# One-core attention and gated-MLP kernel: Q and K loads in two requests each, Q in three fixed buffers, new orders of work, last head's transfers on GpSimd

## The chip, the cores and the metric

The kernel runs on one core of one Trainium2 chip. The metric is the device time of one execution in microseconds (us); the time of before is the median of three runs. One further execution was recorded by the hardware profiler, and it is this one that the rows of the profile describe. The engines are named as the profile names them: PE (TensorE, matmul), DVE (VectorE), ACT (ScalarE), POOL (GpSimd), SP (SyncE, which here only issues transfers). SP's requests are worked off by 16 DMA engines; each request is split over several of them.

## The reference

Two branches work on the same input x (2048 positions, 448 features) and are mixed by a gate of one number per position:

```python
g = sigmoid((x * gate_w).sum(-1, keepdims=True))
# a: attention with 16 heads of 28 features
qkv = (x @ wqkv).reshape(B, S, 3, H, 28).transpose(2, 0, 3, 1, 4)
scores = einsum("bhqd,bhkd->bhqk", q, k) * 28 ** -0.5
a = (softmax(scores) @ v).transpose(0, 2, 1, 3).reshape(B, S, 448) @ wo
# b: MLP with 1792 hidden features
gate, up = x @ W_gate, x @ W_up
b = (where(gate > 0, gate, 0) * up) @ W_down
out = g * a + (1 - g) * b
```

## The kernel before, in words

**Number format.** Every matmul factor is split into a high and a low part, and products are made of several terms of parts. For the scores of a head the terms are stacked as rows: a K buffer has four blocks of 28 rows (high, low, high, low part of K), and a Q buffer has four blocks of 28 rows (high, high, low, low part of Q), each 2048 wide, 8 KB to a row in f32. So one matmul with 112 rows sums four terms. Sixteen more rows carry the subtraction of the row maximum: -1 in K, and in Q two rows of maxima (written late by POOL) and zeros, which are loaded from `z_d`.

**Opening.** The projections to q and k (`qk`, L435) and to v (`vproj`, L453) run as a list of 35 items in alternation. Results go to DRAM, `qk_d` with the high part first and the low part second (outermost index 0 and 1). K and Q of head 0 are loaded ahead of item 0, those of head 1 ahead of item 6. From item `first` = 11 on, `AHEAD` = 102 matmuls of the maximum search for head 0 and 1 are mixed in (`smax`, L240 on PE and L241 on DVE).

**Rounds.** Then come 32 rounds, two to a head. A string of letters (`FIRST`, `SECOND`, `AA`, `BB` and so on) gives the order in which PE is fed in a round: `s` scores of the current head with exp on ACT (L263, L265), `m` maximum search for a head further on (L240, L241), `r` and `d` raw scores and their maxima for the last four key tiles of the next head (L271 to L279), `e` the exp of those, `x` a matmul of the MLP's gate and up projection (L608). The digit is the PSUM bank. PE works strictly in this order: when one `m` has to wait for its K or Q, all that is behind it waits as well.

**Between the rounds.** Behind the second round of head h stand, in this order: `load_k(h + 3)` (L217, four requests of 28 rows), `raw_top(h + 1)` (a maximum made on DVE, L284 to L292, sent to DRAM by `mr_d<-V`, L293, and back to all partitions by `V<-mr_d`, L294), `load_q(h + 3)` (L222, four requests of 28 rows, and L224, sixteen rows of zeros), then the next gate and up weights (`wgr<-wgu`, L316) and v (L639). All of these are issued by SP, which works in order as well: a request that waits for its buffer or its data holds up those behind it. The transfers of one queue are worked off in order on each DMA engine too. A K buffer comes free behind the last scores of its head, a Q buffer likewise. Q buffers come from a pool of three, which two x tiles and the first weight pair share in the opening.

**End.** When the attention is done the last head is normalised (`row_sums`, `spread`, `normalise`, L658 to L675): reciprocals are sent to DRAM, spread back over 32 partitions each, multiplied, and the head's output goes to `o_d`. Then the list `todo` runs the MLP's down projection (`down`, L888) with the attention's output projection (`wout`, L842) and the results mixed in.

Of the kernel before, what the change touches and what calls it, by code (L numbers as in the profile page):

```python
# [9 lines left out]
F32 = mybir.dt.float32  # L10
# [31 lines left out]

AHEAD = 102

# [3 lines left out]

FIRST = ("m2m3m6m7s0s1uxxxxs0xm2lxxxxUs3xs6xm1xxm7s0s2xxxs3m1xm0xxm2r7r3r1xxdr0s2dr7xdxxs3xdr2xs1m0ds3xxm1xm0s"
         "3r2xxm1ds3xm0xxm1xr3xs2m0dxxm1s2xx")  # L50

SECOND = ("xs0m1r2xm6s7dxs3m0xs1m6xs7xm3r2s0xm1dxs6m7xs3m0xs1r6xm2s3dxm7s1xm0s2xr3m1xs7dm2xs0m1xs7xm3r0s2xs7dm1"
          "xm3s2xs0m7xm1xs2r3xm0xds2m1xs0xs2m3xs0m1xr2s3m0xds1xxm3m0s1s2xxm3s1r0m2xm3ds1xs2xxm1xm2s0x")

AA = ("xs0r1m2xs6m7xxm3s0xm1s6xr2s7xm0dxs3m6xxm1s7r0xm3xds2xs6xm7xs1er3m2m0xm7s1exdm2xs0xm1er7xs0m3xdes2xxm"
      "0s1xem3r2xs1xdm0exxs3m1xs2exm0m3xs1m2exs0xr1m3exs2dm0xxs3xm1s2xm0xxr1m2s0d")

# [10 lines left out]

AZ = ("xs0xs1xxs2xxs6xs7xxs3xs0xxs1xxs2xs7xxs3xs0xxs1xxs2xs3xxs0xxs1xes2xxs3xes0xxs1xxes2xs0xxs1xx")

BZ = ("xs0xs1xxs2xxs6xs7xxs3xs0xxs1xxs2exs7xxs3xes0xxs1xxes2xs3xxs0exxs1xs2xexs3xs0xxs1xxs2xs0xxs1xx")

DA = ("xs0m1xr2m6s7xm3xs0xm2r7xs1m6dxs0xm3xs2xs1xm6r0m7xm2s3dxxm1s7xs3r2xm0m7xds3xs1m0xr3m7xs1dxes2m0xxm1xe"
      "s3m2xs0xr1em3xs2dxm0xes3xm2r1xs0em3dxs2xm0exs3xm2s1xem0r3xm2s1dxm0xxm2s1")
# [4 lines left out]
CA = ("xs0xm1s2r6m7xm3xs0xm2r6s1xxdm7s0m3xr2xs1m6dxs0xm7m3xs1xr6xm0xds2m7xs1xr3m0s2xdxm1m7xs0r2xem3s1dxm0s7"  # L79
      "xes3m1xm2xm0exs3r1xxm2des3xm0xs2m3exs1xr2m0exm3ds1xm0xexs3m1xs2xs0xxm2m1s0")  # L80

# [19 lines left out]
def gated_mix_kernel(ctx, tc, x, wq, wo, wgu, wd, out):  # L101
# [82 lines left out]
    K = [vp.tile([P, S], F32R, name=f"K{r}") for r in range(3)]  # L184

    def p_slot(k, name, dt=F32):
        return (vp if k < 5 else att).tile([P, 4, TB], dt, name=name, tag=f"P{k}", bufs=1)
# [3 lines left out]
    def slot(k):  # L191
        if k not in slots:
            slots[k] = p_slot(k, f"P_{k}")
        return slots[k]
# [14 lines left out]

    def q_slot(name):  # L210
        return vp.tile([P, 4, TB], F32R, name=name, tag="Q", bufs=3)

    Q = {}

    def load_k(h):
        for r in range(4):
            nc.sync.dma_start(f32(K[h % 3])[DH * r:DH * (r + 1)], qk_d[r % 2, 2 * DH * h:2 * DH * h + DH, :])  # L217

    def load_q(h):
        Q[h] = q_slot(f"Q_{h}").rearrange("p j t -> p (j t)")  # L220
        for r in range(4):
            nc.sync.dma_start(f32(Q[h])[DH * r:DH * (r + 1)], qk_d[r // 2, 2 * DH * h + DH:2 * DH * (h + 1), :])  # L222

        nc.sync.dma_start(f32(Q[h])[GD:], z_d[0:1].to_broadcast([P - GD, S]))  # L224

# [83 lines left out]
    def fetch_f(i):  # L309

        if i == 0:
            pair.append(vp.tile([P, 4, TB], F32, name="pair", tag="Q", bufs=3))
            WR[i] = pair[0][:, :2].rearrange("p s (c f) -> p s c f", c=4)
        else:
            WR[i] = fe.tile([P, 2, 4, P], F32, name=f"wgr_{i}", tag="wgr", bufs=2)
        nc.sync.dma_start(WR[i], wgu[i % NF])  # L316


    with tc.tile_pool(name="qkv", bufs=1) as pa:
# [75 lines left out]
        for tb in range(NB - 1, 0, -1):  # L395
            X[tb] = tuple(q_slot(f"X{r}_{tb}") if tb + r == NB else p_slot(next(free), f"X{r}_{tb}", F32R)
                          for r in range(2))

# [134 lines left out]
        spills = {15 + 3 * k: (NB - 1 - k // 2, k % 2) for k in range(6)}  # L533
        m, first, ahead = 0, 11, AHEAD
        for n, (f, *a) in enumerate(mixed):
# [105 lines left out]
    def pv(i0, ni, po):  # L641
# [11 lines left out]
        if (i0 + ni) % NK == 0:  # L653
            LS[h] = fe.tile([P, 16], F32, name=f"ls_{h}", tag="ls", bufs=2)
            nc.gpsimd.dma_start(LS[h], OS[h][DH::32].rearrange("j (p c) -> j p c", c=16))

    def row_sums(h):

        r = fe.tile([P, 16], F32, name=f"rs_{h}", tag="rs", bufs=2)
        nc.vector.reciprocal(r, LS.pop(h))  # L660
        nc.sync.dma_start(l_d[h].rearrange("j (p c) -> (j p) c", c=16), r)

    def spread(h):


        LS[h] = fe.tile([P, TB + 8], F32, name=f"rb_{h}", tag="rb", bufs=1)[:, :TB]
        for j in range(NB):
            nc.sync.dma_start(LS[h][32 * j:32 * j + 32], l_d[h][j:j + 1].to_broadcast([32, TB]))

    def normalise(h):  # L670
        o = OS.pop(h)
        engine = nc.gpsimd if h + 1 < H else nc.vector
        engine.tensor_tensor(o, o, LS.pop(h), op=OP.mult)
        for j in range(NB):
            nc.sync.dma_start(o_d[DH * h:DH * (h + 1), j * TB:(j + 1) * TB], o[32 * j:32 * j + DH])  # L675

# [5 lines left out]
    def small_things(h):  # L682

        load_v(h + 1) if h + 1 < H else None
        if h == 0:
            pack_wo()

# [3 lines left out]

    summed = []
    split_f(0, act_high, pool_low, (0,))
# [4 lines left out]
    for r, order in enumerate(ROUNDS):  # L698
# [91 lines left out]
        pv(i0, 8, banks[3])  # L790
    assert raw == NI and m == len(MAXIMA), (raw, m)
    stk.close()

# [22 lines left out]
    def fetch_o(tb):  # L816
        OR[tb] = r = pf.tile([P, 4, TB], F32, name=f"or_{tb}", tag="or", bufs=1)
        t = slice(tb * TB, (tb + 1) * TB)
        nc.sync.dma_start(r[:, 0:3], o_d[0:3 * P, t].rearrange("(c p) t -> p c t", p=P))
        for a in (0, 64):  # L820
            nc.sync.dma_start(r[a:a + 64, 3], o_d[3 * P:, t])

# [92 lines left out]

    todo = [(gate_up, done), (row_sums, H - 1), (gate_up, done + 1)]
    for i in range(NB * NF):
# [7 lines left out]


    before(0, (spread, H - 1))
# [62 lines left out]
```

## Time and profile before

| | |
|---|---|
| median of three runs | 1311.88 us (1309.97 to 1313.3) |
| profiled execution, its time | 1312.3 us |
| its span (first to last instruction) | 1310.5 us |
| PE busy | 1252.3 us, 96% of the span |
| DVE, ACT, POOL busy | 905.4, 841.7, 632.3 us |
| mean granted TensorE clock | 0.980 |
| moved by DMA | 159.14 MB, 121 GB/s on average |

PE is the engine to look at. Its busy time counts the modelled length of matmuls, which overlap, so a short wait of PE shows in the list of waits and in the timeline sooner than in the busy share. In the timeline and the windows, times are microseconds from the start of the span; a window row gives the length, then busy time and count of PE, PEld, DVE, ACT and POOL, then the granted clock (1.00 is full speed), the mean busy share of the 16 DMA engines, and GB/s.

### The profile page before, as it was taken

The page shows a single profiled execution, that of the slowest core. Times are in us where ns is not written, and L with a number is a line of the kernel's source. Part 1 is how long each engine was busy: PE and PEld are TensorE (multiplying, and loading weights), DVE is VectorE, ACT ScalarE, POOL GpSimd, SP SyncE. Part 2 cuts the span into 40 slices and gives each one's busy share as a digit, 9 for nine tenths or more (in the row PEclk, how much of TensorE's full clock was granted, in tenths as well). Part 3 has the DMA queues.
Part 4 walks back from the last instruction along what each step waited for, and adds up shares of the span by engine and source line. Part 5 has one row for each costly group of instructions (what it writes and reads, how often), then busy time and mean ns, then how long its engine had stood idle before and what let it go on. Part 6 is the DMA issues. An engine that isn't in the chain of part 4 may idle for free.

```text
span 1310.5 us, 18847 instructions
## 1 busy us (share of the span) xinstructions
PE 1252.3 (96%) x6447; PEld 865.9 (66%) x6447; DVE 905.4 (69%) x1446; ACT 841.7 (64%) x1661; POOL 632.3 (48%) x698
## 2 busy tenths in 40 slices
PE   9999698999999989998989999998999999899998
PEld 6888565666556655665656566565565565689997
DVE  6498578787777777786858687877687735563332
ACT  5212566878696868877767788686878796322121
POOL 4323225555737383837383737454574577351020
PEclk9999999999999989999989999999999999999999
DMA  8956715151535252424442443517151222744432
GB/s 311 320 199 225 195 68 126 48 125 57 133 94 136 72 118 76 107 86 103 125 116 84 109 90 101 123 52 181 48 126 48 66 65 82 252 148 117 131 114 79
DMA packets 62872, 159.14 MB, mean 121 GB/s; under 512 B 13288, under 2 KB 20024, under 8 KB 58168
## 3 DMA queue, kind: packets, MB, share of 16 engines
q1 hardware_dynamic: 49352, 114.51, 33.2%
q0 software_dynamic: 12992, 42.97, 9.2%
q8 instruction: 50, 0.82, 0.3%
q10 hardware_dynamic: 432, 0.46, 0.1%
q14 instruction: 46, 0.38, 0.1%
HBM read 110.19 MB, written 48.16 MB: 121 GB/s over the span
## 4 chain that ended last, share of the span: by engine, by line
PE 74%; DMA 14%; DVE 4%; ACT 3%; SPq 2%; issue 2%; POOL 1%; ACTq 0%; DVEq 0%; POOLq 0%
PE b L608 16%; PE b L240 12%; PE b L646 12%; PE b L263 11%; PE b L888 9%; DMA wgr<-wgu 8%; PE b L435 5%; PE b L271 3%; PE b L842 3%; PE b L453 3%; DMA mr_d<-V 2%; ACT P L265 2%; DMA K<-qk_d 1%; DVE V L290 1%; SPq L222 1%
## 5 line engine op out<-in xcount | busy, mean ns | idle before, releaser
L241 DVE TENSOR_REDUCE mx<-b 128x1 f32<-128x512 f32 x784 | 519.7, 685 | 101.3 <-PE b L240 95.4
L265 ACT ACTIVATE P<-b 128x512 f32<-128x512 f32 x780 | 446.8, 606 | 191.2 <-PE b L263 179.4
L608 PE MATMUL b<-X,wg 128*128 128x512 f32 (+1 forms) x1232 | 436.8, 405 | 0.2 <-POOL wg L161 0.2
L240 PE MATMUL b<-K,Q 128*128 128x512 f32 x784 | 314.8, 408 | 44.7 <-DMA wgr<-wgu 39.7
L263 PE MATMUL b<-Q,K 128*128 128x512 f32 x784 | 316.8, 406 | 0.7 <-ACT P L265 0.5
L608 PEld LDWEIGHTS b<-X,wg 128*128 128x128 f32 (+1 forms) x1232 | 224.1, 191 | 63.2 <-issue 22.6
L646 PE MATMUL b<-P,v 128*32 128x512 f32 x1800 | 226.2, 594 | 0.0
L240 PEld LDWEIGHTS b<-K,Q 128*128 128x128 f32 x784 | 149.7, 192 | 95.5 <-issue 47.1
L630 POOL DMA_DIRECT2D h_d<-rl x56 | 31.5, 562 | 329.9 <-DVE rl L624 281.4
L263 PEld LDWEIGHTS b<-Q,K 128*128 128x128 f32 x784 | 149.5, 191 | 57.2 <-ACT P L265 22.8
L298 POOL TENSOR_TENSOR P<-P,V 128x512 f32<-128x512 f32 x120 | 150.3, 1286 | 42.7 <-DMA V<-mr_d 42.7
L298 POOL TENSOR_TENSOR V<-V 128x512 f32<-128x512 f32 x120 | 150.1, 1286 | 22.3 <-DMA V<-mr_d 22.3
L161 POOL TENSOR_TENSOR wg<-wgr,wg 128x384 fp32r<-128x384 f32 x216 | 155.1, 732 | 9.5 <-DVE wg L155 0.9
L646 PEld LDWEIGHTS b<-P,v 128*32 128x32 f32 x1800 | 61.7, 110 | 144.5 <-issue 143.4
L279 DVE TENSOR_TENSOR V<-b,V 128x512 f32<-128x512 f32 x215 | 146.5, 681 | 6.0 <-ACT V L275 3.9
L888 PE MATMUL b<-WD,hh 128*128 128x448 f32 x672 | 143.5, 372 | 7.2 <-ACT hh L152 5.3
L888 PEld LDWEIGHTS b<-WD,hh 128*128 128x128 f32 x672 | 127.7, 190 | 21.3 <-ACT hh L152 5.7
L152 ACT ACTIVATE hh<-hr 128x512 fp32r<-128x512 f32 x56 | 35.4, 632 | 129.6 <-PE b L888 113.8
L646 PE MATMUL b<-V,v 128*32 128x512 f32 x248 | 110.1, 593 | 0.0
L271 PE MATMUL b<-Q,K 128*128 128x512 f32 x240 | 97.8, 409 | 0.2
L158 DVE TENSOR_TENSOR hh<-hr,hh 128x512 fp32r<-128x512 f32 x56 | 51.5, 920 | 62.0 <-ACT hh L152 62.0
L435 PE MATMUL b<-X,W 128*128 128x512 f32 x308 | 82.7, 394 | 0.1
(91 smaller groups left out, 1110.2 us busy)
## 6 DMA issues: line engine op xcount, KB each, us to landing
wgr<-wgu SPq DMA_DIRECT2D x55, 512.0 KB
K<-qk_d SPq DMA_DIRECT2D x64, 224.0 KB
Q<-qk_d SPq DMA_DIRECT2D x64, 224.0 KB
h_d<-rl POOLq DMA_DIRECT2D x56, 256.0 KB, 3.0
hr<-h_d SPq DMA_DIRECT2D x56, 256.0 KB
qk_d<-st POOLq DMA_DIRECT2D x21, 512.0 KB, 5.9
x_d<-X POOLq DMA_DIRECT2D x6, 1024.0 KB, 5.8
X<-x_d SPq DMA_DIRECT2D x24, 256.0 KB
```

Source lines behind the costliest of these rows:

```text
L161: nc.gpsimd.tensor_tensor(dst, src, f32(high), op=OP.subtract)
L240: nc.tensor.matmul(ps, Q[h][:, u * P:(u + 1) * P], K[h % 3][:, c * TB:(c + 1) * TB], start=True, stop=True)
L241: nc.vector.tensor_reduce(MX[h][:, 4 * u + c:4 * u + c + 1], ps, axis=AX.X, op=OP.max)
L263: nc.tensor.matmul(ps, K[h % 3][:, kt * P:(kt + 1) * P], Q[h][:, j * TB:(j + 1) * TB], start=True, stop=True)
L265: nc.scalar.activation(prob(i, j), ps, AF.Exp, scale=SCALE)
L271: nc.tensor.matmul(ps, K[h % 3][:, kt * P:(kt + 1) * P], Q[h][:, 3 * TB:], start=True, stop=True)
L279: nc.vector.tensor_tensor(run, ps, run if i % NK > 1 else prob(i - 1, 3), op=OP.max)
L298: nc.gpsimd.tensor_tensor(own, own, piece(TOP), op=OP.subtract)
L435: nc.tensor.matmul(ps, W[:, a, c * P:(c + 1) * P], xf(tb, b), start=(n == 0), stop=(n == NT - 1))
L608: nc.tensor.matmul(ps, WS[i][rows, s, a], xf(i // NF, b)[rows], start=(n == 0), stop=(n == NT - 1))
L646: nc.tensor.matmul(po[32 * j:32 * j + 32], VH[h][:, i % NK], prob(i, j), start=(i == i0), stop=(i == i0 + ni - 1))
L888: nc.tensor.matmul(ACC[i // NF][t][:, :D], HH[i][:, a, t * P:(t + 1) * P], WD[:, f, b], start=(f == 0 and n == 0), stop=(f == NF - 1 and n ...
```

## The change

**K and Q requests.** `load_k` and `load_q` make two requests of 56 rows where there were four of 28. For K, the outermost index of the source runs over the high and the low part; for Q it is a repetition with stride zero.

```diff
     def load_k(h):
-        for r in range(4):
-            nc.sync.dma_start(f32(K[h % 3])[DH * r:DH * (r + 1)], qk_d[r % 2, 2 * DH * h:2 * DH * h + DH, :])
+        for a in (0, 2):
+            nc.sync.dma_start(f32(K[h % 3])[DH * a:DH * (a + 2)], qk_d[:, 2 * DH * h:2 * DH * h + DH, :])
 
     def load_q(h):
-        Q[h] = q_slot(f"Q_{h}").rearrange("p j t -> p (j t)")
-        for r in range(4):
-            nc.sync.dma_start(f32(Q[h])[DH * r:DH * (r + 1)], qk_d[r // 2, 2 * DH * h + DH:2 * DH * (h + 1), :])
-
-        nc.sync.dma_start(f32(Q[h])[GD:], z_d[0:1].to_broadcast([P - GD, S]))
+        Q[h] = QB[h % 3].rearrange("p j t -> p (j t)")
+        for a in range(2):
+            nc.sync.dma_start(f32(Q[h])[2 * DH * a:2 * DH * (a + 1)],
+                              qk_d[a:a + 1, 2 * DH * h + DH:2 * DH * (h + 1), :].to_broadcast([2, DH, S]))
+
+        n = P - GD if h < 3 else 2
+        nc.sync.dma_start(f32(Q[h])[GD:GD + n], z_d[0:1].to_broadcast([n, S]))
```

The access patterns that these lines make, as [stride, count] from the outermost in: one K request reads [[1835008, 2], [2048, 28], [1, 2048]], one Q request [[0, 2], [2048, 28], [1, 2048]], and both write 56 rows of 2048. Before, each read and wrote [[2048, 28], [1, 2048]].

**Buffers.** The three Q buffers are fixed (`QB`), and the first weight pair moves to another slot.

```diff
+    QB = [vp.tile([P, 4, TB], F32R, name=f"Q{r}") for r in range(3)]
...
-            slots[k] = p_slot(k, f"P_{k}")
+            slots[k] = p_slot((0, 1, 2, 3, 5, 6, 7, 4, 8)[k], f"P_{k}")
...
-            pair.append(vp.tile([P, 4, TB], F32, name="pair", tag="Q", bufs=3))
+            pair.append(p_slot(4, "pair"))
```

**Opening.** Head 2's K and Q move from the letter `u` of the first round into the opening; the search starts one item earlier, with two matmuls fewer.

```diff
-        m, first, ahead = 0, 11, AHEAD
+        m, first, ahead = 0, 10, AHEAD
...
-            if n == len(mixed) - 6:
+            if n == len(mixed) - 7:
+                load_k(2)
+                load_q(2)
+            if n == len(mixed) - 3:
                 fetch_f(0)
...
                 split_f(0, act_high, pool_low, (1,))
-                load_k(2)
-                load_q(2)
                 fetch_f(2)
```

**Weights and V.** `fetch_f` at the rounds' end and `load_v` go into a list that is written out behind the eighth `s` of the next round (the output weights too, behind the eighth `s` of head 1).

```diff
             if parts % 2 == 0 and parts // 2 + 1 < NB * NF:
-                fetch_f(parts // 2 + 1)
+                later.append((fetch_f, parts // 2 + 1))
...
                     rest.pop(0)()
+                if ns == 8:
+                    while later:
+                        f, *a = later.pop(0)
+                        f(*a)
```

**Orders.** `AHEAD` becomes 100, and the strings `FIRST`, `SECOND`, `AA`, `AZ`, `DA` and `CA` are new; `AA`, `DA` and `CA` are first rounds of a head.

**The last head.** `row_sums`, `spread` and `normalise` of head 15 and the first block of attention output are issued by POOL instead of SP; `spread` stands right behind `row_sums` in the list.

```diff
+    def side(h):
+        return nc.sync if h + 1 < H else nc.gpsimd
...
-        nc.sync.dma_start(l_d[h].rearrange("j (p c) -> (j p) c", c=16), r)
+        side(h).dma_start(l_d[h].rearrange("j (p c) -> (j p) c", c=16), r)
...
-        high = WO[:, c if c < 3 else 6]
-        dve_high(high, wor[:, c])
+        act_high(high, wor[:, c])
...
-            early = i < 6
+            early = i < 8
...
-    todo = [(gate_up, done), (row_sums, H - 1), (gate_up, done + 1)]
+    todo = [(gate_up, done), (row_sums, H - 1), (spread, H - 1), (gate_up, done + 1)]
...
-    for tb, load, split, at in ((0, 2, (6, 7), (10, 11, 12, 13)), (1, 8, (12, 14), (17, 18, 19, 20)), (2, 21, (23, 25), (28,) * 4),
+    for tb, load, split, at in ((0, 2, (8, 9), (10, 11, 12, 13)), (1, 8, (12, 14), (17, 18, 19, 20)), (2, 21, (23, 25), (28,) * 4),
...
-    for c in range(4):
-        todo.insert(todo.index((down, c)), (split_wo, c))
+    todo[3:3] = [(split_wo, c) for c in range(4)]
...
-        if n in (2, 3):
-            split_d(n - 2)
+        if n in (7, 8):
+            split_d(n - 7)
```

**What moves on the engines.** SP behind the second round of head 0, before: K of head 3, the raw maximum out and back, Q of head 3, its zeros, two halves of weights, v of head 2.

```order
L217 DMA K0_127<-qk_d_77 28x2048 x4
L293 DMA mr_d_1_86<-V_126 16x32
L294 DMA V_126<-mr_d_1_86 128x512
L222 DMA Q_3_1663<-qk_d_77 28x2048 x4
L224 DMA Q_3_1663<-z_d_101 16x2048
L316 DMA wgr_6_1677<-wgu 128x1024
L316 DMA wgr_7_1687<-wgu 128x1024
L639 DMA v_2_1729<-v_d_84 128x512
```

The same place of the change:

```order
L216 DMA K0_127<-qk_d_77 56x1x2048 x2
L294 DMA mr_d_1_86<-V_126 16x32
L295 DMA V_126<-mr_d_1_86 128x512
L221 DMA Q0_130<-qk_d_77 56x1x2048 x2
L225 DMA Q0_130<-z_d_101 2x2048
L317 DMA wgr_6_1767<-wgu 128x1024
L317 DMA wgr_7_1769<-wgu 128x1024
L642 DMA v_2_1771<-v_d_84 128x512
```

The order on SP is the same; the K and Q requests are two of 56 rows in place of four of 28, and the zeros are two rows in place of sixteen.

SP in the opening, of the change, from the first K on (before, the three requests of K2 and Q2 stood behind the weight pair, one further weight, the v of heads 0 and 1 and the output weights):

```order
L216 DMA K0_127<-qk_d_77 56x1x2048 x2
L221 DMA Q0_130<-qk_d_77 56x1x2048 x2
L225 DMA Q0_130<-z_d_101 16x2048
L216 DMA K1_128<-qk_d_77 56x1x2048 x2
L221 DMA Q1_131<-qk_d_77 56x1x2048 x2
L225 DMA Q1_131<-z_d_101 16x2048
L216 DMA K2_129<-qk_d_77 56x1x2048 x2
L221 DMA Q2_132<-qk_d_77 56x1x2048 x2
L225 DMA Q2_132<-z_d_101 16x2048
L317 DMA pair_1082<-wgu 128x1024
L317 DMA wgr_1_1183<-wgu 128x1024
L642 DMA v_0_1185<-v_d_84 128x512
```

Head 2's requests now stand ahead of the first weights.

PE around the first maximum matmul of head 4 (K1 with Q of head 4), in the first round of head 2, before:

```order
L240 MATMUL b_1_70<-K0_127,Q_3_1663 128x512
L271 MATMUL b_7_76<-Q_3_1663,K0_127 128x512
L608 MATMUL b_5_74<-X0_120,wg_7_2161 128x512
L263 MATMUL b_0_69<-Q_2_1222,K2_129 128x512
L240 MATMUL b_3_72<-K1_128,Q_4_2155 128x512
L608 MATMUL b_6_75<-X0_120,wg_8_2171 128x512
```

The same place of the change:

```order
L272 MATMUL b_1_70<-Q0_130,K0_127 128x512
L611 MATMUL b_5_74<-X0_120,wg_7_2134 128x512
L264 MATMUL b_2_71<-Q2_132,K2_129 128x512
L241 MATMUL b_3_72<-K0_127,Q0_130 128x512
L611 MATMUL b_6_75<-X0_120,wg_8_2142 128x512
L264 MATMUL b_7_76<-Q2_132,K2_129 128x512
L611 MATMUL b_6_75<-X0_120,wg_8_2142 128x512
L241 MATMUL b_0_69<-K0_127,Q0_130 128x512
L611 MATMUL b_6_75<-X1_121,wg_8_2142 128x512
L264 MATMUL b_2_71<-Q2_132,K2_129 128x512
L241 MATMUL b_3_72<-K1_128,Q1_131 128x512
```

Here the first one stands one gate-and-up unit later: between the last matmul that reads the K buffer for its old head and the first one that reads it for head 4 PE has 93 matmuls instead of 86. Over the 13 heads from 3 to 15 there are 56 matmuls more in these gaps.

More of the change, by code (lines that the diff above doesn't have):

```diff
@@ L40 @@
 EARLY = (5, 5, 4, 4, 4, 3, 3, 3, 2, 2, 2, 2, 1, 1, 1, 1)
[L43 to L56, printed above, removed]
+AHEAD = 100
+FIRST = ("m2m3m6m7s0s1uxxxxs0xm2lxxs3xm6xUxs1xm7xs0m2xxm3xs1xxs0m7m2s1xr3r0r7m1xdr2xdr3xdxr1s0dxxdxxxm2m0s3xxm"
+         "1xm3r2xxm0xdm1xxs3xs0xxm2r3s0m1xdxs2s0m1m2m0m1")
+SECOND = ("xs0m1r2xs6m7dxs3xm0s1xm6s7xr3s2xm1dxs0m7xs6xm2s1r0xs3m6dxs7xm1s2xm3r7xs0xds2m1xs3m0xs7xm2r1s3xm0ds7x"
+          "xs2m3xs0r1m2xs3dxm0xs2s3xm1xs2r0m3xs1dm2xxs3m1xs0xs3r2xm1s0dm3xxxs1m0s2xxm1xs2")
+AA = ("xm0s1xr2m6s7xm3xs1xm2s7xr0m6xs1dxm3s7xm2xr6s1m0xdxs7m3xs2m1xr0exm7s3dxm2s1exm7xs3xm0er1xs2m3dxes7xm0"
+      "xs2m3er1xxs0m2dxes3xxm0m2xes1r3xm0xxdes2m1xs0xem3s2xm1s0xm3r2xs1m0dxxxs1m0")
 BB = ("xm0s1r2xm7s6dxxm3s1xm0xs7r6xm2s1dxm3xs0xm7r2s1xm6dxs0xm3xs7m1xr0s2xm3dxs7m1xs2xm3xr7m0s2xdxm1s3xm2s0"
@@ L395, in gated_mix_kernel @@
         for tb in range(NB - 1, 0, -1):
-            X[tb] = tuple(q_slot(f"X{r}_{tb}") if tb + r == NB else p_slot(next(free), f"X{r}_{tb}", F32R)
-                          for r in range(2))
+            X[tb] = tuple(QB[2] if tb + r == NB else p_slot(next(free), f"X{r}_{tb}", F32R) for r in range(2))
         def split_x(tb, raw):
@@ L667, in spread @@
         for j in range(NB):
-            nc.sync.dma_start(LS[h][32 * j:32 * j + 32], l_d[h][j:j + 1].to_broadcast([32, TB]))
+            side(h).dma_start(LS[h][32 * j:32 * j + 32], l_d[h][j:j + 1].to_broadcast([32, TB]))
     def normalise(h):
@@ L674, in normalise @@
         for j in range(NB):
-            nc.sync.dma_start(o_d[DH * h:DH * (h + 1), j * TB:(j + 1) * TB], o[32 * j:32 * j + DH])
+            side(h).dma_start(o_d[DH * h:DH * (h + 1), j * TB:(j + 1) * TB], o[32 * j:32 * j + DH])
     def pack_wo():
@@ L682, in small_things @@
     def small_things(h):
-        load_v(h + 1) if h + 1 < H else None
-        if h == 0:
-            pack_wo()
+        if h + 1 < H:
+            later.append((load_v, h + 1))
+        if h == 1:
+            later.append((pack_wo,))
     def short(r):
         return r >= len(ROUNDS) - 4
-    summed = []
+    summed, later = [], []
     split_f(0, act_high, pool_low, (0,))
@@ L791, in gated_mix_kernel @@
     assert raw == NI and m == len(MAXIMA), (raw, m)
+    for f, *a in later:
+        f(*a)
     stk.close()
@@ L818, in fetch_o @@
         t = slice(tb * TB, (tb + 1) * TB)
-        nc.sync.dma_start(r[:, 0:3], o_d[0:3 * P, t].rearrange("(c p) t -> p c t", p=P))
+        queue = nc.sync if tb else nc.gpsimd
+        queue.dma_start(r[:, 0:3], o_d[0:3 * P, t].rearrange("(c p) t -> p c t", p=P))
         for a in (0, 64):
-            nc.sync.dma_start(r[a:a + 64, 3], o_d[3 * P:, t])
+            queue.dma_start(r[a:a + 64, 3], o_d[3 * P:, t])
     def split_o(tb, c):
@@ L924, in before @@
         todo[n:n] = new
-    before(0, (spread, H - 1))
     before(1, (normalise, H - 1))
-    for tb, load, split, at in ((0, 2, (6, 7), (10, 11, 12, 13)), (1, 8, (12, 14), (17, 18, 19, 20)), (2, 21, (23, 25), (28,) * 4),
+    for tb, load, split, at in ((0, 2, (8, 9), (10, 11, 12, 13)), (1, 8, (12, 14), (17, 18, 19, 20)), (2, 21, (23, 25), (28,) * 4),
                                 (3, 35, (37, 39), (42,) * 4)):
```

12 lines of the change are left out of this document (5 added, 7 removed).

## The prediction

> **What bounds the kernel now.** I read the busy table first, then the chain that ended last, then PE's waits, then SP's and PE's timelines around those waits.
>
> ```profile
> PE 1252.3 (96%) x6447; PEld 865.9 (66%) x6447; DVE 905.4 (69%) x1446; ACT 841.7 (64%) x1661; POOL 632.3 (48%) x698
> PE 74%; DMA 14%; DVE 4%; ACT 3%; SPq 2%; issue 2%; POOL 1%; ACTq 0%; DVEq 0%; POOLq 0%
> ```
>
> PE is busy for 96% of the span and no other engine for over 69%; yet DMA owns 14% of the chain. So the bound is PE, with places where a transfer ends last. The waits name them:
>
> ```profile
> PE b L240 <- DMA wgr<-wgu: 39.7, 10, 10.9
> PE b L888 <- ACT hh L152: 5.3, 1, 5.3
> PE b L240 <- DMA Q<-z_d: 4.2, 1, 4.2
> ```
>
> A maximum matmul (L240) needs K and Q and no weights: `wgr` is merely the transfer that the trace saw landing next, and the sixteen zero rows in the last line are Q's own. So 39.7 + 4.2 = 43.9 us of PE waits are waits for a new head's K and Q, eleven times, 10.9 of them once (head 2) and 33.0 in the other ten. At the handover to the down projection (L888) PE waits 5.3 once more.
>
> SP's timeline for head 3, then the start of PE's wait-ended matmul; then the same for head 14:
>
> ```profile
> 207.11 1.62 SPq L217 DMA_DIRECT2D K<-qk_d  x4
> 213.84 0.31 SPq L293 DMA_DIRECT2D mr_d<-V  x1
> 215.56 0.34 SPq L294 DMA_DIRECT2D V<-mr_d  x1
> 216.02 1.63 SPq L222 DMA_DIRECT2D Q<-qk_d  x4
> ```
>
> ```profile
> 227.38 1.19 PE L240 MATMUL b<-K,Q 128*128 128x512 f32 x2 [3.56 <-DMA wgr<-wgu]
> 914.92 0.47 PE L240 MATMUL b<-K,Q 128*128 128x512 f32 x1 [4.22 <-DMA Q<-z_d]
> ```
>
> ```profile
> 891.86 1.87 SPq L217 DMA_DIRECT2D K<-qk_d  x4
> ```
>
> From K's issue to PE's restart is 20.3 us for head 3 (227.38 - 207.11) and 23.1 for head 14; over the eleven heads of 3 to 15 where PE waits or nearly waits for it (first and last of them shown) the mean is 21.0. Of head 3's 20.3, SP's chain of K, maximum out, maximum back takes 8.9 until Q is issued, and Q needs 11.4 to arrive. PE has on average 18 us of other matmuls for this time: a longer transfer lengthens every head, and a shorter one gains 3 us a head at most.
>
> **The change part by part.** *K and Q in two requests.* What matters is over how many DMA engines a request is spread. Windows of the trace: only K's 28-row requests in the first, 128-row requests in the third, both Q and weights in the second.
>
> ```profile
> 212.00:213.00 1.00, 1.00 (x12) 0.26 (x8) 0.97 (x3) 0.00 (x0) 0.92 (x2) 1.00 0.87 193
> 226.00:228.00 2.00, 0.62 (x2) 0.56 (x3) 0.25 (x1) 0.00 (x0) 2.00 (x3) 0.50 0.93 344
> 75.00:77.00 2.00, 2.00 (x11) 1.80 (x10) 1.95 (x4) 0.56 (x2) 0.71 (x1) 1.00 0.93 371
> ```
>
> The DMA share of 0.87 is 14 engines of 16 (0.875): a 28-row request leaves two idle although it has rows enough for all. 14 is the largest number up to 16 that divides 28. So the outermost count of the request sets the engines. The new requests have 56 rows on the SBUF side, but the outermost count of the source is 2 (high and low part for K, the repetition for Q). If the count that divides both sides is taken, two engines carry all of K, and the same two all of Q. No row of before has such a request; I take two engines, because the row shows that the rows aren't simply dealt out over 16.
>
> The Trainium skill says this as a rule: in "DMA: Bandwidth & Descriptors", section "Why a DMA increments its semaphore by 16 and not by 1", the number of engines is the largest one up to 16 that divides the slowest dimension of both access patterns, and "Rules for kernel authors" there warns of an outermost repetition of few copies. The 0.87 of the first window agrees for 28; for 2 no row here can show it. By the opposite reading the time would be that of the first rival.
>
> The price of an 8 KB row on one engine has two bounds: 371 GB/s over 16 x 0.93 engines is 24.9 GB/s each, so 0.33 us; 193 over 16 x 0.87 is 13.9, so 0.59 us. Two engines are far from loading memory as sixteen do, so I take 0.33 (the second window gives 0.35).
>
> ```profile
> 207.00:208.00 1.00, 1.00 (x10) 0.39 (x12) 0.66 (x2) 0.81 (x2) 0.00 (x0) 1.00 0.00 0
> ```
>
> Then, from K's issue (time 0):
>
> - first data at +1 (the window from 207 to 208 still shows a DMA share of 0.00); each engine has 2 requests x 28 rows = 56 rows, 18.5 us: K lands at +19.5, where now it does not end last.
> - `mr_d<-V` is issued at +6.7 as now, but its pieces on those two engines queue behind K: out of DRAM at about +20.5, when `V<-mr_d` can go, against +8.5 now (215.56 - 207.11). Its 2 KB rows add 16 KB = 0.7 to each engine: +22.2 with the issue between.
> - Q's 56 rows an engine, 18.5: +40.7. Zeros, one row an engine, 0.3: +41.0. 1.5 for the last landing and PE's restart: +42.5.
>
> That is 21.5 more than the 21.0 of now, in 13 heads: **+279.5 us**. PE's 18 us of cover stays as it is; behind the waiting maximum stand scores, gate and up matmuls, so ACT, DVE and POOL all stop with it, and POOL's subtraction waits for V some 12 us longer within the same time.
>
> Three heads have x loads ahead in the queue; their K and their returning maximum:
>
> ```profile
> 390.48 2.44 SPq L217 DMA_DIRECT2D K<-qk_d  x4
> 401.16 0.34 SPq L294 DMA_DIRECT2D V<-mr_d  x1
> 641.25 2.45 SPq L217 DMA_DIRECT2D K<-qk_d  x4
> 654.27 0.34 SPq L294 DMA_DIRECT2D V<-mr_d  x1
> 903.45 0.34 SPq L294 DMA_DIRECT2D V<-mr_d  x1
> ```
>
> Here the maximum comes back 10.7, 13.0 and 11.6 (from 891.86) after K, for head 3 it was 8.5. The excess, 10 us in all, is older transfers that K must wait for: **+10**.
>
> *New orders.* They put 56 matmuls more between K's issue and the first maximum. Those are done inside the wait, and so they are missing after it. From the chain,
>
> ```profile
> 9.09 30.83 PE b L435 x133
> ```
>
> a matmul is worth 30.83 / 133 = 0.23 us: **-13**. The strings else hold the same matmuls.
>
> *Opening.* K0 is issued first at
>
> ```profile
> 37.60 2.54 SPq L217 DMA_DIRECT2D K<-qk_d  x4
> 40.18 1.87 SPq L222 DMA_DIRECT2D Q<-qk_d  x4
> L240 PE MATMUL b<-K,Q x784: 387/393/767, 56.9 to 1036.1; 128*128 128x512 f32 x196
> ```
>
> and PE comes to the first maximum at 56.9 without a wait; one item earlier that is about 54. K0 and Q0 are 112 rows an engine: 38.6 + 37 = 75.6, with 5 of sharing with the stores of the opening and 1.5 at the end 82: **+28**. K1 and Q1 then need 37 more in the same engines, while work for 37 is about there: +5 (0 to 10). The weight pair for the first round now queues behind K2 and Q2, another 37 us on two engines: +5 (-3 to 13). Against it, head 2's wait of 10.9 goes, since its K and Q are issued in the opening already:
>
> ```profile
> 165.00 0.76 PE L240 MATMUL b<-K,Q 128*128 128x512 f32 x1 [10.90 <-DMA wgr<-wgu]
> ```
>
> with 1.5 of slow clock behind it. Opening in sum: **+26**.
>
> *Clock.* After a wait the granted clock is halved for some microseconds: 0.50 in the window 226 to 228, and still at
>
> ```profile
> 231.00:232.00 1.00, 1.00 (x4) 0.81 (x3) 0.43 (x1) 0.41 (x2) 1.00 (x2) 0.50 0.46 129
> core 0: 1310.5 us, clock 0.980
> ```
>
> From the restart at 227.4 to 232 that costs half, 2.3 us. The mean of 0.980 leaves 26 us missing over the span, of which some 18 fall after restarts and the rest into waits. With 14 long waits of 2 us each I count 28: **+10**.
>
> *Weights and V behind the eighth score.* SP's order of requests is the same as before, and SP waits for buffers and data, not for PE's scores: 0. If a weight did come later, POOL's split and the matmuls behind it would wait,
>
> ```profile
> PE b L608 <- POOL wg L161: 0.2, 1, 0.2
> ```
>
> where now one wait of 0.2 us is seen; the wait for Q would cover it, and without that cover it costs what the weight is late. Fixed Q buffers: Q[h+3] takes the buffer that the pool gave, 0 (-1 to 1). Zeros in 2 rows for 16: one row an engine less or none, inside the 0.3 above.
>
> *Handover.* POOL issues the last head's transfers, so SP's weights don't stand behind them; `WO`'s high parts go from DVE to ACT and come earlier.
>
> ```profile
> 1130.14 7.22 PE L888 MATMUL b<-WD,hh 128*128 128x448 f32 x34 [1.04 <-DVE hh L158]
> 1142.65 10.18 PE L888 MATMUL b<-WD,hh 128*128 128x448 f32 x37 [5.29 <-ACT hh L152]
> 1153.73 2.54 PE L888 MATMUL b<-WD,hh 128*128 128x448 f32 x11 [0.91 <-POOL WD L161]
> ```
>
> All three waits are 7.2 and cost some 2.5 of slow clock: at best -10, at worst +5 if POOL, which now waits for DVE's reciprocals in order, delays its low parts; nearer to the best: **-8**.
>
> Sum: 279.5 + 10 - 13 + 26 + 10 - 8 = +304.5. On the span of 1310.5 that is 1615.0; the profiled execution has 1.8 us outside its span (1312.3 - 1310.5), so **1617 us**. That execution lies 0.4 above the median of the runs, so nothing is to be corrected.
>
> **The rivals.** *Wide.* The 56 rows on the SBUF side alone set the engines, 14 as now. Then transfers land as they do, and the change gains: four requests are issued in place of eight (K and Q x4 take 1.6 each, so Q is on its way 0.8 earlier), 56 / 13 = 4 matmuls more before each first maximum (1.0): 1.8 off each of eight waits and the two short ones gone, 16 in all:
>
> ```profile
> 288.94 0.47 PE L240 MATMUL b<-K,Q 128*128 128x512 f32 x1 [0.48 <-DVE mx L241]
> 788.85 0.47 PE L240 MATMUL b<-K,Q 128*128 128x512 f32 x1 [0.84 <-DMA wgr<-wgu]
> ```
>
> To this come head 2's 10.9 and its 1.5; half of the 18 of slow clock, 8 (waits under 3 us leave less of it); 5 at the handover. 1312.3 - 41.4 = 1271 us (1246 to 1292). For it: 28 divides 56 too, and the trace cannot say that the source counts. Against it: a request that reads 2 x 28 has to be cut on the reading side as well. This one is on the other side of no change, and it decides from the number of engines alone: at two engines slower, at 14 faster; by the price above, some five engines would be even.
>
> *Narrow and slow.* Two engines, but 0.59 us a row, if a row of 8 KB is what is slow in K's loads and not memory. K and Q are then 33 each, the restart at +72.5, +51.5 in 13 heads = 670; the opening 30 more than above, and the rest as above: about 2040.
>
> *Narrow, on engines of their own.* Q's requests go to other engines than K's, or the maximum is not held up: then the maximum returns at +8.5, Q is issued at +9 and its 18.5 end at +28.5, with the end +30: +9 in 13 heads = 117, the opening about 18 less: 1312.3 + 117 + 10 - 13 + 8 + 10 - 8 = 1436. The trace shows one queue for all of SP's transfers, so I hold it unlikely.
>
> **How the numbers follow.** Two engines shared by K and Q, at 0.33: 0.78. Wide: 0.12. Narrow and slow: 0.04. Own engines: 0.05. The remaining 0.01 is no change, if few engines and the gains should balance. The forecast's own range is 1500 (0.29 a row, 112 rows x 0.04 = 4.5 a head less, 58, and 4 a head less where K's rows let the maximum pass sooner, 52) to 1720 (0.40 a row: 112 x 0.07 = 7.8 a head more, 102). The range for 8 in 10 takes in the case of own engines below: 1430 to 1720. Over 0.3% is about what a measurement of this kernel can tell from no change (4 us). Faster 0.12, within 0.3% 0.01, slower 0.87.
>
> **What will show it.** If right: SP's timeline shows `V<-mr_d` some 20 us after K's issue where it is 8.5 now; in the stretch between K's issue and PE's restart the DMA share falls to about 2/16 = 0.13; PE's waits at the maximum matmul are some 23 us, thirteen times, in place of 43.9 in all; the first one in the opening ends near 82; PEclk falls to 0.50 once a head. The handover shows fewer than 7.2 us of waits, or else that term is wrong. The prediction is wrong if the share in K's stretch stays at 0.87 and PE's waits shrink (wide), if the waits grow to 50 us (slow rows), or if Q's issue stays at +9 while waits grow (own engines).

## The result, and the profile after

The changed kernel takes 1672.77 us (median of four runs, 1668.19 to 1674.2), against 1310.93 us of the kernel before beside it: a ratio of 1.275 (95% interval 1.272 to 1.279), slower. The profiled execution has a span of 1670.6 us, 360.1 longer than before.

The busy table, the first part of the chain and the list of DMA issues of the page after answer to the lines shown of before:

```profile
PE 1274.1 (76%) x6447; PEld 885.9 (53%) x6447; DVE 897.8 (54%) x1442; ACT 848.2 (51%) x1667; POOL 628.9 (38%) x708
...
PE 52%; DMA 36%; DVE 5%; issue 2%; ACT 2%; SPq 1%; POOL 1%; DVEq 0%; ACTq 0%; POOLq 0%
...
K<-qk_d SPq DMA_DIRECT2D x32, 448.0 KB
```

PE does the same 6447 matmuls, but its share falls from 96% to 76%: of the 360 us some 338 are time in which PE is not busy, and 22 are longer busy time for the same count of matmuls (mean granted clock 0.879, before 0.980). K is now loaded by half as many requests of twice the size. DMA's share of the chain goes from 14% to 36%. PE's waits after (engine and line, waited for what: us in all, times, longest):

```profile
PE b L241 <- DMA Q<-z_d: 309.6, 13, 29.9
PE b L264 <- ACT P L266: 46.6, 6, 12.2
PE b L264 <- DMA Q<-mh: 14.3, 1, 14.3
PE b L241 <- DMA Q<-qk_d: 12.2, 1, 12.2
...
PE b L900 <- DVE WD L158: 2.5, 1, 2.5
```

The maximum matmul (L241 now) waits 309.6 + 12.2 us for Q, the first wait of the opening (29.9) included, where 43.9 us were waited before. Five of the six waits of L264 for ACT come in heads in which a shorter wait for Q follows (the sixth is 0.5 us); there PE stops earlier, at a score, and restarts no later than in the other heads. Both together PE waits some 26 us in each of the thirteen heads; the prediction said some 23. The two waits of the opening that are new are looked at below. At the handover (L900) 2.5 us are left of 7.2.

SP's timeline for head 3, and PE's restart:

```profile
251.62 1.26 SPq L216 DMA_DIRECT2D K<-qk_d  x2
258.17 0.33 SPq L294 DMA_DIRECT2D mr_d<-V  x1
273.55 0.33 SPq L295 DMA_DIRECT2D V<-mr_d  x1
274.33 1.27 SPq L221 DMA_DIRECT2D Q<-qk_d  x2
```

```profile
297.05 0.76 PE L241 MATMUL b<-K,Q 128*128 128x512 f32 x1 [28.20 <-DMA Q<-z_d]
```

The maximum is sent off 6.6 us after K as before, but it is back only 21.9 us after K (8.5 before), and Q takes 22.7 from issue to restart (11.4 before). A window between the two, in which only K's rows are under way:

```profile
260.00:270.00 10.00, 8.86 (x39) 6.87 (x37) 9.87 (x19) 7.35 (x13) 1.60 (x3) 1.00 0.14 53
```

The DMA share is 0.14, some two engines of 16, and they move 53 GB/s.

### The profile page after: what moved, and what is told of

It is laid out like the page before. It is cut to its first block, busy times and chain, and to the rows that moved or that the text cites. A ratio compares the mean times of both kernels' runs of the same rounds, so it can differ in the third digit from the quotient of the medians.

```text
span 1670.6 us, 18735 instructions
## 1 busy us (share of the span) xinstructions
PE 1274.1 (76%) x6447; PEld 885.9 (53%) x6447; DVE 897.8 (54%) x1442; ACT 848.2 (51%) x1667; POOL 628.9 (38%) x708
## 3 DMA queue, kind: packets, MB, share of 16 engines
q1 hardware_dynamic: 46260, 111.46, 20.8%
## 4 chain that ended last, share of the span: by engine, by line
PE 52%; DMA 36%; DVE 5%; issue 2%; ACT 2%; SPq 1%; POOL 1%; DVEq 0%; ACTq 0%; POOLq 0%
DMA Q<-z_d 18%; DMA mr_d<-V 13%; PE b L611 12%; PE b L264 8%; PE b L241 8%; PE b L900 8%; PE b L649 7%; PE b L272 3%; PE b L435 2%; DMA qk_d<-st 2%; PE b L854 2%; DVE V L291 2%; DMA Q<-qk_d 1%; DMA Q<-mh 1%; SPq L221 1%
## 5 line engine op out<-in xcount | busy, mean ns | idle before, releaser
L241 PE MATMUL b<-K,Q 128*128 128x512 f32 x784 | 323.7, 417 | 326.9 <-DMA Q<-z_d 309.6
L611 PE MATMUL b<-X,wg 128*128 128x512 f32 (+1 forms) x1232 | 443.8, 412 | 0.0
L264 PE MATMUL b<-Q,K 128*128 128x512 f32 x784 | 320.8, 411 | 61.1 <-ACT P L266 46.6
L241 PEld LDWEIGHTS b<-K,Q 128*128 128x128 f32 x784 | 154.7, 198 | 379.2 <-issue 327.7
L611 PEld LDWEIGHTS b<-X,wg 128*128 128x128 f32 (+1 forms) x1232 | 229.7, 196 | 65.4 <-issue 21.3
L264 PEld LDWEIGHTS b<-Q,K 128*128 128x128 f32 x784 | 153.0, 195 | 114.6 <-ACT P L266 66.7
L900 PE MATMUL b<-WD,hh 128*128 128x448 f32 x672 | 142.4, 371 | 2.5 <-DVE WD L158 2.5
L900 PEld LDWEIGHTS b<-WD,hh 128*128 128x128 f32 x672 | 127.3, 190 | 16.0 <-DVE WD L158 2.9
L303 ACT ACTIVATE P<-P 128x512 f32<-128x512 f32 x120 | 71.7, 634 | 77.5 <-POOL P L299 77.4
L276 ACT ACTIVATE V<-b 128x512 f32<-128x512 f32 x116 | 69.5, 604 | 67.8 <-PE b L272 66.4
L272 PE MATMUL b<-Q,K 128*128 128x512 f32 x240 | 100.4, 420 | 0.2
```

The source lines that it names most:

```text
L241: nc.tensor.matmul(ps, Q[h][:, u * P:(u + 1) * P], K[h % 3][:, c * TB:(c + 1) * TB], start=True, stop=True)
L264: nc.tensor.matmul(ps, K[h % 3][:, kt * P:(kt + 1) * P], Q[h][:, j * TB:(j + 1) * TB], start=True, stop=True)
L272: nc.tensor.matmul(ps, K[h % 3][:, kt * P:(kt + 1) * P], Q[h][:, 3 * TB:], start=True, stop=True)
L303: nc.scalar.activation(own, own, AF.Exp, scale=SCALE)
L611: nc.tensor.matmul(ps, WS[i][rows, s, a], xf(i // NF, b)[rows], start=(n == 0), stop=(n == NT - 1))
L900: nc.tensor.matmul(ACC[i // NF][t][:, :D], HH[i][:, a, t * P:(t + 1) * P], WD[:, f, b], start=(f == 0 and n == 0), stop=(f == NF - 1 and n ...
```

## The experiments

Three theories stood against each other. **A**: the outermost count of a request sets its number of DMA engines; 2 means two engines, and that is all of the loss. **B**: requests of 56 rows, or their sources (two far parts, a repetition), are slow in themselves. **C**: the new orders and moved requests cost a good part. All times stand beside runs of the kernel before on the same chip (medians 1308.3 to 1310.1 us). The runs of three groups stand on three chips; differences between groups are better read from the ratios to before.

**Only the requests put back.** The edit to the changed kernel (Q likewise):

```diff
-        for a in (0, 2):
-            nc.sync.dma_start(f32(K[h % 3])[DH * a:DH * (a + 2)], qk_d[:, 2 * DH * h:2 * DH * h + DH, :])
+        for r in range(4):
+            nc.sync.dma_start(f32(K[h % 3])[DH * r:DH * (r + 1)], qk_d[r % 2, 2 * DH * h:2 * DH * h + DH, :])
```

> The changed kernel with only the K and Q requests put back to four of 28 rows each. Theory A (an outermost count of 2 puts a request on two DMA engines, and that is all of the loss): K and Q land as before the change, the wait of head 2 in the opening is gone, and the time is 1250 to 1290 us, faster than before. Theory B (requests of 56 rows are slow whatever the order of their dimensions): the same time here. Theory C (the new orders of work or the moved requests cost most of the loss): it stays above 1400 us.

Measured: 1257.27 us, a ratio to before of 0.961 (0.958 to 0.964). C falls: without the new requests the rest of the change is a gain of 4%.

**The same two requests, other order of dimensions.**

```diff
-            nc.sync.dma_start(f32(K[h % 3])[DH * a:DH * (a + 2)], qk_d[:, 2 * DH * h:2 * DH * h + DH, :])
+            nc.sync.dma_start(f32(K[h % 3])[DH * a:DH * (a + 2)],
+                              qk_d[:, 2 * DH * h:2 * DH * h + DH, :].rearrange("a d s -> d a s"))
...
-                              qk_d[a:a + 1, 2 * DH * h + DH:2 * DH * (h + 1), :].to_broadcast([2, DH, S]))
+                              qk_d[a:a + 1, 2 * DH * h + DH:2 * DH * (h + 1), :].rearrange("a d s -> d a s")
+                              .to_broadcast([DH, 2, S]))
```

> The changed kernel with its two 56-row requests for K and for Q kept, but their source read with the 28 rows as the outermost count and the high and low part (or the repetition) inside. The rows of a block then stand in another order in both K and Q, the products are the same. Theory A: 14 engines again, DMA share near 0.87 in K's stretch, 1250 to 1290 us, within 10 us of the four-request kernel. Theory B (56 rows in a request are slow in themselves, or the source's two far parts are): it stays near 1670 us.

Measured: 1248.0 us, 0.954 (0.951 to 0.956), just below the expected range and 9 us faster than with four requests. The source patterns are [[2048, 28], [1835008, 2], [1, 2048]] and [[2048, 28], [0, 2], [1, 2048]]; rows, bytes, requests, far parts and repetition are those of the change, and 425 us are gone. B falls. A window inside K's transfer, and PE's waits for Q in this kernel:

```profile
197.00:199.00 2.00, 2.00 (x24) 0.61 (x20) 1.97 (x4) 2.00 (x6) 1.54 (x3) 1.00 0.87 221
```

```profile
PE b L243 <- DMA Q<-qk_d: 1.6, 1, 1.6
...
PE b L243 <- DMA Q<-z_d: 0.6, 2, 0.4
```

The share is 0.87 again, and the waits for Q are 2.2 us in all.

**K alone, and Q alone, in the form of the change.**

> The changed kernel with only Q put back to four requests of 28 rows; K keeps its two requests with outermost count 2. Theory A with one order of transfers on each engine: K still holds up the returning maximum until +22 us from its issue, Q is issued at +22.4 and needs 11.2 as before the change, so the restart is at about +33.6, some 14 us a head later than with four requests, 1430 to 1480 us in all. Rival (K is not on the path, since its engines let the small transfers pass): the maximum returns at +8.5 and the time is within 30 us of the four-request kernel.

> The changed kernel with only K put back to four requests of 28 rows; Q keeps its two requests with outermost count 2, a repetition with stride zero. Theory A: the maximum returns at +8.5 us from K's issue, Q is issued at +9 and needs 22.7 as in the changed kernel, so the restart is at about +31.6, some 12 us a head later than with four requests, 1410 to 1460 us. Rival (the repeated read with stride zero is what is slow, K in two requests costs nothing): most of the whole loss stays, above 1580 us.

Measured: 1461.41 us with K's two requests, as expected, and 1475.81 us with Q's, above the expected 1410 to 1460. Head 3 in the first (SP, then PE):

```profile
224.46 1.28 SPq L216 DMA_DIRECT2D K<-qk_d  x2
231.01 0.34 SPq L293 DMA_DIRECT2D mr_d<-V  x1
245.99 0.34 SPq L294 DMA_DIRECT2D V<-mr_d  x1
246.38 1.69 SPq L221 DMA_DIRECT2D Q<-qk_d  x4
```

```profile
255.88 0.76 PE L240 MATMUL b<-K,Q 128*128 128x512 f32 x1 [14.15 <-DMA wgr<-wgu]
```

and in the second:

```profile
224.65 1.62 SPq L216 DMA_DIRECT2D K<-qk_d  x4
231.20 0.31 SPq L294 DMA_DIRECT2D mr_d<-V  x1
232.82 0.34 SPq L295 DMA_DIRECT2D V<-mr_d  x1
233.20 1.26 SPq L221 DMA_DIRECT2D Q<-qk_d  x2
```

```profile
256.49 0.76 PE L241 MATMUL b<-K,Q 128*128 128x512 f32 x1 [14.60 <-DMA Q<-z_d]
```

In the first the maximum needs 15.0 us from `mr_d<-V` to `V<-mr_d`, in the second 1.6: PE does not wait for K's data, it waits because the small transfer of the maximum stands behind K in the same engines. Q then takes 9.5 from issue to restart; in the second 23.3. In the second the restart is at +31.8, where +31.6 was expected; what was taken too small is the loss against the four-request kernel, which restarts at +17.8 and not near +20. Over four plain requests the losses are 204 and 219 us, 423 together; the change with both loses 1672.8 - 1257.3 = 416. The two parts add up to within 7 us.

**The kernel before with the change's requests alone.**

> The kernel before with only its K and Q requests made two of 56 rows each with outermost count 2, as in the change. Theory A (these requests are all of the loss, and the rest of the change gains some 50 us when K and Q land in time): every head's restart comes some 25 us later, 12 periods of head 3 to 15 give 310, head 2, the opening and the end 25 each, 1660 to 1720 us, slower than the change itself. Rival (orders and moved requests cost a part of the loss by themselves): under 1620 us.

Measured: 1708.39 us, 1.306 (1.302 to 1.311). This is 36 us above the whole change: the rest of the change gains here too, less than the 51 (1308.3 - 1257.3) that it gains with four requests. As the transfers are the same in both, this kernel serves below to tell apart what the orders and the clock are worth.

**Four and seven engines.** Four plain requests, the 28 rows of each read as 4 x 7 or 7 x 4 (Q in the same order):

```diff
-            nc.sync.dma_start(f32(K[h % 3])[DH * r:DH * (r + 1)], qk_d[r % 2, 2 * DH * h:2 * DH * h + DH, :])
+            nc.sync.dma_start(f32(K[h % 3])[DH * r:DH * (r + 1)], qk_d[r % 2, 2 * DH * h:2 * DH * h + DH, :]
+                              .rearrange("(n m) s -> m n s", m=4))
```

> The changed kernel with four requests of 28 rows for K and for Q whose source reads the 28 rows as 4 x 7, outermost 4 (rows in another order, the same in K and Q). Theory A, the outermost count sets the engines: four engines carry K and Q, 28 rows each at 0.33 to 0.35 us, the maximum returns at about +12.5 us from K, the restart is at about +26, some 6 us a head later than with 14 engines: 1310 to 1370 us, DMA share near 0.25 in K's stretch. Rival (what costs is two far parts or a repetition in one request): 1250 to 1265 us as with four plain requests.

> The same with the 28 rows read as 7 x 4, outermost 7. Theory A: seven engines, 16 rows each, K over before the maximum is made, Q in about 9 us: nothing lost against 14 engines, 1240 to 1265 us, DMA share near 0.44 in K's stretch. Rival (the number of engines in use is the limit all along): twice the transfer time of 14 engines, over 1290 us.

Measured: 1415.85 us with 4 outermost and 1300.24 us (ratio 0.993, 0.990 to 0.996) with 7. A window inside K's transfer of each, 4 first:

```profile
218.00:222.00 4.00, 4.00 (x22) 2.60 (x15) 3.93 (x7) 1.98 (x4) 3.04 (x5) 1.00 0.25 103
```

```profile
206.00:208.00 2.00, 2.00 (x24) 0.39 (x12) 1.90 (x6) 0.00 (x0) 1.93 (x4) 1.00 0.43 170
```

The shares are 4/16 = 0.25 and 7/16 = 0.44: with 0.14 for 2 and 0.87 for 14 this is the outermost count each time. The rule that the prediction named, from the Trainium skill ("DMA: Bandwidth & Descriptors", section "Why a DMA increments its semaphore by 16 and not by 1"), agrees with all four. The times were both missed: 1416 against 1310 to 1370, 1300 against 1240 to 1265. PE's restart for head 3 shows by how much:

```profile
240.23 0.77 PE L242 MATMUL b<-K,Q 128*128 128x512 f32 x1 [11.84 <-DMA wgr<-wgu]
```

```profile
221.39 0.49 PE L242 MATMUL b<-K,Q 128*128 128x512 f32 x1 [3.61 <-DMA Q<-qk_d]
```

That is 29.1 us after K's issue with four engines (K at 211.12; 26 expected) and 20.8 with seven (K at 200.55; 17.8 with fourteen). So each is some 3 us a head later than was reckoned; why is not shown. With four engines the loss was also counted from a restart at +20, where fourteen reach +17.8. And the time with seven lies in the range of the rival (over 1290): the number of engines is still a limit there, though the transfer does not take twice as long as with fourteen.

**What the rest of the change gains.** First the kernel before with only the good two requests:

> The kernel before with two 56-row requests for K and for Q with the 28 rows as the outermost count, and nothing else of the change. If halving the requests brings Q 1.5 to 2 us earlier in each head, the eleven waits of PE shrink by that: 1275 to 1295 us. If the gain of the changed kernel with good requests comes from the orders and the opening instead, it stays within 8 us of before.

Measured: 1285.74 us, 0.984 (0.981 to 0.987): the transfers alone bring 23 us. Its waits at the maximum matmul:

```profile
PE b L243 <- DMA Q<-z_d: 25.6, 9, 9.0
```

The longest of them, 9.0, is still that of head 2 (10.9 before).

Then, from the 1248 us kernel, one part at a time taken back.

```diff
     def side(h):
-        return nc.sync if h + 1 < H else nc.gpsimd
+        return nc.sync
...
-        queue = nc.sync if tb else nc.gpsimd
+        queue = nc.sync
```

> The changed kernel with the 28 rows outermost, and the last head's transfers and the first block of attention output issued by SP again, not POOL; the other edits of the handover stay. If POOL's issuing is what shortens the handover: 3 to 8 us slower than the 1248 us with POOL. If the earlier weights and the moved splits do it: within 3 us of it.

Measured: 1251.78 us, 0.955 (0.953 to 0.957), against 0.954 (0.951 to 0.956): not told apart by the times. In the one profiled execution of each, the span behind head 15's K grows from 348.2 to 351.4 us, and the down projection waits 4.0 us for ACT again.

```diff
-                later.append((fetch_f, parts // 2 + 1))
+                fetch_f(parts // 2 + 1)
...
-        if h + 1 < H:
-            later.append((load_v, h + 1))
-        if h == 1:
-            later.append((pack_wo,))
+        load_v(h + 1) if h + 1 < H else None
+        if h == 0:
+            pack_wo()
```

> The changed kernel with the 28 rows outermost, and weights and V asked for at the rounds' end in the program's order, not behind the eighth score. SP's order of requests should hardly change, so within 3 us of the 1248 us. Rival (their place behind K and Q matters): over 5 us slower.

Measured: 1249.24 us, 0.954 (0.951 to 0.956): nothing. SP's order hardly changes: in each head the weights that are issued ahead of K move from behind the stores of attention output (`o_d<-os`) to ahead of them, as in the kernel before.

```diff
-            if n == len(mixed) - 7:
-                load_k(2)
-                load_q(2)
...
                 split_f(0, act_high, pool_low, (1,))
+                load_k(2)
+                load_q(2)
                 fetch_f(2)
```

> The changed kernel with the 28 rows outermost, and the K and Q of head 2 loaded in the first round again (at the letter u), not in the opening. The prediction's term is 10.9 us of wait and 1.5 of slow clock; with requests that land 2 us sooner 7 to 13 us slower than 1248 us. If the time is the same, the wait was hidden in the first round's other limits.

Measured: 1253.58 us, 0.957 (0.955 to 0.960): 5.6 us by the medians, 4.6 by the ratios, less than the expected 7 to 13. The wait of head 2:

```profile
157.90 1.19 PE L243 MATMUL b<-K,Q 128*128 128x512 f32 x2 [3.67 <-DMA Q<-z_d]
```

```diff
-AHEAD = 100
+AHEAD = 102
...
-        m, first, ahead = 0, 10, AHEAD
+        m, first, ahead = 0, 11, AHEAD
```

and the six strings of before:

> The changed kernel with the 28 rows outermost, and the strings, AHEAD and first item of before. The new strings leave 56 more matmuls ahead of the first maxima; with the old ones short waits come back in some heads: 5 to 15 us slower than 1248 us. If Q lands early enough in any case: within 4 us.

Measured: 1254.03 us, 0.957 (0.955 to 0.959): 6.0 us by the medians, 4.6 by the ratios. These last two losses are 0.35% by the ratios, with intervals that overlap that of the 1248 us kernel: at the edge of what can be told.

## Why the prediction was right, and where its sizes were off

**Two engines for K and Q: right.** The share, the late return of the maximum, the wait in every head and the sign came as worked out, and the kernels with 28 outermost, K alone and Q alone show the cause. That K and Q have the same two engines is seen in the opening: the first maximum waits until 84.36, as K and Q of head 0 one after the other on two engines would make it (82 said), and from 64 to 84 the DMA share is 0.13. Wide (1271 us, 1246 to 1292) is what the change would have been with 28 outermost: 1248.

**The forecast of 1617 was 56 us short**, inside its range of 1430 to 1720. The span falls into three pieces at the issues of K for head 3 and head 15. Those of before and after:

```profile
953.60 1.73 SPq L217 DMA_DIRECT2D K<-qk_d  x4
```

```profile
1295.69 1.25 SPq L216 DMA_DIRECT2D K<-qk_d  x2
```

- *Up to head 3's K*: 207.11 to 251.62, +44.5, forecast about +27 (26, and 1 of the clock's 10). The first wait was well priced: it ends at 84.36 (82 said). The terms for what follows, +5 and +5, were too small:

```profile
84.36 0.76 PE L241 MATMUL b<-K,Q 128*128 128x512 f32 x1 [29.91 <-DMA Q<-z_d]
140.22 0.79 PE L241 MATMUL b<-K,Q 128*128 128x512 f32 x1 [4.70 <-DVE mx L242]
174.25 0.76 PE L264 MATMUL b<-Q,K 128*128 128x512 f32 x1 [14.32 <-DMA Q<-mh]
```

  The last wait is the one that was left out. It is for no load of K or Q, but for POOL's write of head 0's maxima into Q, a row to each request. The chain of the opening:

```profile
139.87 15.14 DMA qk_d<-st
...
155.58 18.54 DMA Q<-mh
```

  The small write took 18.5 us and a store of the projections 15.1, where the median of these stores was 5.9 before and is 8.3 after (the page before, then the page after):

```profile
qk_d<-st POOLq DMA_DIRECT2D x21, 512.0 KB, 5.9
qk_d<-st POOLq DMA_DIRECT2D x21, 512.0 KB, 8.3
```

  SP issued Q of head 2 at 152.23, just ahead of the write, and its 56 rows an engine at 0.33 are 18.5 us: the size agrees with a write that stands behind them, though no row names the engine that carried it. I had counted who queues behind K and Q on SP, and not what POOL sends through the same engines.

- *Head 3's K to head 15's*: 746.5 to 1044.1, +297.6, forecast about 265 (12 x 21.5 + 10 - 12 of the orders + 9 of the clock). The restart comes on average 45.8 us after K, over the thirteen heads, where 42.5 and 0.8 for the x loads were said: 2.5 a head, 30 in the twelve periods. Of the 2.5, 0.9 is K and the maximum (back at 22.2, 21.3 said), and 1.6 is Q (23.2 from issue to restart, 21.5 said). The price of a row was right: 53 GB/s over 0.14 x 16 engines is 23.7 GB/s, 0.35 us for 8 KB, and a window inside head 4's Q gives 25.0, 0.33 us:

```profile
370.00:375.00 5.00, 0.00 (x0) 0.00 (x0) 0.00 (x0) 0.05 (x1) 5.00 (x5) 0.91 0.13 52
```

  At 0.35 the 112 rows cost 2.2 us more than at 0.33, at 0.33 nothing, so how much of the 2.5 is the row and how much the start and end of a transfer stays open. Stores of POOL do fall into K's transfer (`h_d<-rl`, issued at 253.73 in head 3). The weights that SP issues behind Q don't seem to delay it: in head 4 PE restarts at 382.06, and the two engines go on until 384.5, about the time that their share of the weights and v takes.

- *Behind it*: 356.9 to 374.9, +18.0, forecast about 12.5 (21.5 for the last head, -1, -8).

The other terms:

- **Clock** (+10): the mean of 0.879 was mostly lost inside waits, where it costs nothing. What it costs outside is seen in the kernel before with the change's requests alone, which has the orders of before: from PE's restart to the next head's K it takes 462.6 us over the eleven heads of 3 to 14 in which the kernel before waits too; that one takes 454.0, so 0.8 a head and about 10 over thirteen, as forecast.
- **Orders** (-13): the same stretch, over twelve periods, is 506.1 us in that kernel and 492.8 in the change: -13.3, where -12 of the -13 was said. The orders are not the only difference between these two kernels, so this is an estimate; in the 1248 us kernel, where little is waited for, the orders are worth 5 or 6.
- **Head 2 in the opening** (-12.4 in the wide case): 5 or 6. Good requests alone bring its wait from 10.9 to 9.0 us; loaded in the first round of the 1248 us kernel it waits 3.7. There its K is issued at 141.35, ahead of the output weights, and its Q at 143.48, right behind; in the kernel before with good requests they go at 146.24 and 154.59. So most of the old wait was the place among SP's requests and the gap ahead of Q, and the move into the opening had only the rest to gain. What SP waits for in this gap was not followed up; the fixed Q buffers, counted as 0, may be what closes it.
- **Handover** (-8): behind head 15's K the kernel before with good requests needs 354.7 us and the 1248 us kernel 348.2, so 6.5, of which POOL's issuing is about half (3.2, by one profiled execution of each); the wait named before, for ACT, is the one that went.
- **Eighth score** (0): 0.
- **Zeros in two rows** (inside 0.3): the wide kernel with the old orders restarts some 8.6 us after Q's issue, the kernel before with the same requests 9.5, so this may be worth most of 1 us a head; it was not tried by itself.

In the narrow and slow rival's sum the restart comes out at +71.6 and not +72.5, 12 us less in all, which changes nothing.

**The rivals.** Narrow and slow fell with the row's price, own engines with K alone: the maximum was held up for 15 us. The point where wide and narrow meet was put at five engines; four give +8%, seven are 0.7% faster, so it lies between, nearer to seven.

One thing stays open: two requests with 28 outermost are 9 us faster than four of 28 rows. PE's waits for K and Q are 10.8 us with four and 2.2 with two, so these waits are nearly all of it; why the data are there sooner was not found. At head 3 the restart comes 9.6 us after Q's issue with two and 9.5 with four; later PE restarts 9.5 to 10.1 us after the issue with four, and with two 8.2 and 8.9 in the two heads where it still waits. SP takes as long to issue two (1.68 us) as four:

```profile
204.56 1.68 SPq L222 DMA_DIRECT2D Q<-qk_d  x2
```

so it is not the saved issue that the wide rival named.

## What to carry to other kernels

Before merging DMA requests, look at the outermost count of the access patterns, that of the DRAM side and of a stride-zero repetition included: merging four requests of 28 into two of 2 x 28 cut the engines from 14 to 2 here, and swapping the two dimensions turned a loss of 28% into a gain of 4.6%. Then price everything else that passes through the same engines, small transfers above all: with K alone on two engines the kernel lost 204 us to a returning maximum, nearly as much as with Q alone (219). Where a wait is for data, ask in the profile whether it is the data's own transfer or one ahead of it.

## What the runs showed of the hardware that was not expected

An 8 KB row of K or Q costs an engine the same with two, four and seven engines at work: the windows above give 52 GB/s over 0.13 x 16 engines, 103 over 0.25 x 16 and 170 over 0.43 x 16, which is 25 to 26 GB/s an engine and 0.32 to 0.33 us a row. With fourteen, in the kernel with four plain requests, it costs more:

```profile
197.00:199.00 2.00, 2.00 (x24) 0.57 (x20) 1.97 (x4) 2.00 (x6) 1.09 (x2) 1.00 0.87 209
```

209 GB/s over 14 are 14.9 GB/s each, 0.55 us. Seven times the engines moved K only four times as fast, and seven engines (170 GB/s, some other traffic included) came within a fifth of fourteen. The number of engines alone is not the reason, since requests of 128 rows kept sixteen at 25 GB/s each (371 GB/s at a share of 0.93 in the prediction's third window); what is was not tried. And transfers issued by POOL are not out of reach of SP's: a single row of maxima took 18.5 us, about the time that SP's load of Q just ahead of it kept two engines busy.
